# Moving some stationary operands by 128 bytes in SBUF, in a channel attention with a feed-forward layer

## The chip, the cores and the metric

The kernel runs on one core of a Trainium2 chip. The metric is the device time of one execution in microseconds (us). Before the change three runs gave 2107.0 us as their median, from 2104.4 to 2107.66.

## The reference

Two layers follow one another. The first is a channel attention: q, k and v are 4 batches of 6080 tokens by 256 channels. The second is a feed-forward layer with the square of a ReLU, of 256 channels and 2048 hidden ones, over all 24320 tokens.

```python
qn = q / (np.linalg.norm(q, axis=1, keepdims=True) + 1e-06)
kn = k / (np.linalg.norm(k, axis=1, keepdims=True) + 1e-06)
s = kn.transpose(0, 2, 1) @ qn / tau          # 256 x 256 per batch
a = np.exp(s - s.max(-1, keepdims=True))
a /= a.sum(-1, keepdims=True) + 1e-09
x = v @ a
h = np.maximum(x @ w_in, 0.0)
out = h * h @ w_out
```

The weights w_in and w_out come as 64-bit floating-point numbers, the rest as 32-bit ones.

## The kernel before

**Arithmetic.** Large products are made with the type fp32r, and each 32-bit operand is split into a high part and a low part; a product is three matmuls: high by high, high by low, low by high. Names ending in _hi and _lo are such parts. Since v @ a @ w_in is v @ (a @ w_in), each batch first makes its own W = a @ w_in, and the tokens then go through W, ReLU, square and w_out. The channels lie on the partitions, the tokens along the columns, so in the main loop weights are the stationary operand and tokens the moving one.

**Tiling.** A batch is 12 blocks of tokens: ten of 512 and two of 480. From the third block of the first batch on, both big products go by a scheme of two by two blocks with fewer products (like Strassen's), so that one matmul has half a block as columns: 256, or 240 in the last two blocks of a batch. The forms of W that it needs (with sums and differences of blocks) are kept in DRAM and loaded per group as the tiles wf. For w_out the plain blocks are read from wo_hi and wo_lo, and the sums from wS_hi, wS_lo (even pairs), wS_odd_hi, wS_odd_lo (odd pairs) and some blocks of wo that are overwritten. v is loaded as seven blocks in one tile (`load_v_blocks`, line 821): the places T1, B11, T3, B21, B22, T2, T4 are numbers 0 to 6 (line 986). In a tile of 240 columns they are 960 bytes apart, in one of 256 columns 1024.

**Order.** The loop over groups (four groups to a block of tokens, 512 hidden channels each) calls `period` (line 1331), which goes through the list PERIOD (line 1278): products with wf into the accumulators ps_b, ps_h and ps_c (`product`, line 991, six matmuls on one block of v), and between them the products with w_out of the two groups before into ps_o: `window_S` (line 1063) and `window_A` (line 1058). Every engine runs its instructions in the order of the program. ScalarE evicts, squares and makes high parts; VectorE adds, subtracts and makes low parts; both work beside TensorE. Beside the main loop, at places that `side` names, the attention of the next batch runs: its Gram matrix k-transposed by q (`Gram.products`, line 467; q and k split by `rounded_qk`, line 144, 12 matmuls to a chunk), its softmax (line 649) and its W, a product in which the exponentials eT are the stationary operand (line 751).

**Places in SBUF.** Pools are laid out one behind the other: smalls, const (with wo_hi, wo_lo), wpool (wf), wsums, pool. Within a pool each tag has its room, in the order in which the tags are first asked for. From wo_hi to the end of wsums all rooms are multiples of 1024 bytes per partition, and each begins at 192 modulo 256: wo, wf, wS (8192 bytes each part), wi_hi and wi_lo (4096 each, later the room of wS_odd), eT (2048 each). The first room of pool is that of the parts of q and k (`parts_room`, line 129), two halves of 4096 bytes with a gap between: `rounded_qk` puts k's parts into the first half, and q's parts HALF + GAP words behind them. With a gap of 64 bytes (line 127) the second half and all that follows in pool begin at 0 modulo 256: x, the loads of q and k, acc and dec (which later also hold w_in for the product with eT), A_hi and A_lo, v and its parts, s1 and s2 parts. So in the main loop the stationary operand begins at 192 and the moving one at 0 modulo 256, except that the blocks of 240 columns begin where multiples of 960 bytes fall. wsums holds these tags in this order: wS_hi, wS_lo, wi_hi, wi_lo, eT_hi, eT_lo.

Of the kernel before, what the change touches and what calls it, by code (L numbers as in the profile page):

```python
# [10 lines left out]
F32 = mybir.dt.float32  # L11
# [21 lines left out]
def kernel(  # L33
# [26 lines left out]
    P = 128  # L60
# [40 lines left out]
    wsums = ctx.enter_context(tc.tile_pool(name="wsums", bufs=1))  # L101
# [22 lines left out]
    rinv_room = const.tile([P, NC], F32, name="rinv_room")  # L124

    HALF = NC * GRP
    GAP = 16

    def parts_room(name, dt):

        return pool.tile([P, 2 * HALF + GAP], dt, tag="qk_parts", name=name, bufs=1)

    scalar.activation(parts_room("first", F32)[:, 0:1], exp_bias, AF.Square)
    wo_hi = const.tile([P, NF, C], F32R, name="wo_hi")
    wo_lo = const.tile([P, NF, C], F32R, name="wo_lo")
    late = {}

    def two_parts(name, dt, shape):

        room = parts_room(name, dt)  # L140
        halves = room[:, 0:HALF], room[:, HALF + GAP :]
        return [half.rearrange("p (a b) -> p a b", a=shape[1]) if len(shape) > 2 else half for half in halves]

    def rounded_qk(name):
# [3 lines left out]
        for at in (0, J * C):  # L148
            of_k = room[:, at : at + J * C]
            both = bass.AP(of_k.tensor, of_k.offset, [of_k.ap[0], [HALF + GAP, 2], of_k.ap[1]])  # L150
            parts.append(both.rearrange("p a (j c) -> p a j c", j=J))
# [1435 lines left out]
```

## Time and profile before

| | before |
|---|---|
| median of 3 runs | 2107.0 us (2104.4 to 2107.66) |
| profiled execution: its own time | 2107.39 us |
| its span | 2105.6 us |
| TensorE matmul busy | 2100.4 us (100%), 17158 instructions |
| VectorE busy | 1905.2 us (90%) |
| ScalarE busy | 1879.6 us (89%) |
| GpSimd busy | 350.2 us (17%) |
| DMA, mean | 261 GB/s |

The span runs from the first to the last instruction of the profiled execution, 1.8 us less than the execution's own time. Busy time is the sum of an engine's instructions without overlaps. Matmuls are pipelined, and a row gives one about 0.28 us though the next starts well before that is over; so what counts is the distance from one matmul's start to the next one's, which the chain of waits and the timeline give. The profile shows no addresses; those above are worked out from the sizes of the tiles and the order in which they are asked for.

### The profile page before, as it was taken

Reading aid. Unit: us, or ns where it says so; the run is one execution under the profiler, and the core shown is the slowest. Engines: PE = TensorE matmul, PEld = TensorE weight load, DVE = VectorE, ACT = ScalarE, POOL = GpSimd, SP = SyncE. Lnnn points to the kernel's source line nnn. Section 1 sums busy time; section 2 is a strip of 40 time slices with the busy share of each in tenths; the row PEclk is TensorE's granted clock in tenths of the full one; section 3 lists DMA queues with packets and bytes.
Section 4 is the critical chain, followed back from the end, with each engine's and each line's share of the span. In section 5 each row is a group of like instructions: output and inputs, shape, how many; then the busy total and the mean of one; then the engine's idle time right before and its main releaser. Section 6 shows DMA issues by size and latency. Waiting matters only on the chain.

```text
span 2105.6 us, 43463 instructions
## 1 busy us (share of the span) xinstructions
PE 2100.4 (100%) x17158; PEld 2065.7 (98%) x17158; DVE 1905.2 (90%) x2195; ACT 1879.6 (89%) x2379; POOL 350.2 (17%) x430
## 2 busy tenths in 40 slices
PE   9999999999999999999999999999999999999999
PEld 8789999999999999999999999999999999999999
DVE  7898999989999999989998999998999888888887
ACT  5888999889999999889989999998988988988987
POOL 0000111111121111111122111211111121121112
PEclk9999999999999999999999999999999999999999
DMA  9777888789999888788999978878999787787775
GB/s 357 224 230 274 247 267 250 243 253 309 307 278 317 257 247 255 237 253 281 292 299 277 308 251 260 247 243 248 287 278 304 233 239 246 235 242 243 232 242 154
DMA packets 258012, 549.78 MB, mean 261 GB/s; under 512 B 26672, under 2 KB 113072, under 8 KB 257808
## 3 DMA queue, kind: packets, MB, share of 16 engines
q1 hardware_dynamic: 201456, 469.02, 65.0%
q0 software_dynamic: 56352, 77.98, 18.6%
q8 instruction: 135, 2.21, 0.4%
q14 instruction: 69, 0.57, 0.1%
HBM read 433.59 MB, written 58.72 MB: 234 GB/s over the span
## 4 chain that ended last, share of the span: by engine, by line
PE 99%; ACT 0%; DVE 0%; issue 0%; DVEq 0%; ACTq 0%
PE ps_o L29 45%; PE ps_c L29 18%; PE ps_h L29 14%; PE ps_b L29 12%; PE gram L29 7%; PE ps_w L29 2%; PE ps_end L29 0%; PE ps_first L29 0%; PE ps_n L29 0%; ACT x L29 0%; PE ps_t L29 0%; DVE x L29 0%; DVE w_lo L29 0%; ACT A_hi L29 0%; ACT ps_c L29 0%
## 5 line engine op out<-in xcount | busy, mean ns | idle before, releaser
L29 PE MATMUL ps_c<-v_hi,wf 128*128 128x256 f32 (+1 forms) x2208 | 477.1, 279 | 0.3 <-DVE x L29 0.2
L29 DVE TENSOR_TENSOR x<-x 128x1024 f32<-128x1024 f32 (+2 forms) x549 | 464.9, 847 | 11.1
L29 POOL DMA_DIRECT2D o<-o x225 | 232.6, 1188 | 1401.6 <-ACT o L29 903.4
L29 DVE TENSOR_TENSOR s_lo<-x,s_hi 128x1024 fp32r<-128x1024 f32 (+1 forms) x366 | 441.2, 1207 | 16.6 <-ACT s_hi L29 16.2
L29 ACT ACTIVATE x<-x 128x1536 f32<-128x1536 f32 (+4 forms) x384 | 405.2, 1055 | 42.5 <-DVE x L29 38.9
L29 ACT CAST s_hi<-x 128x1024 fp32r<-128x1024 f32 (+1 forms) x366 | 382.3, 1044 | 50.1 <-DVE x L29 49.1
L29 DVE TENSOR_TENSOR A_lo<-x,A_hi 128x1536 fp32r<-128x1536 f32 (+2 forms) x183 | 313.5, 1713 | 83.1 <-ACT A_hi L29 75.0
L29 PEld LDWEIGHTS ps_c<-v_hi,wf 128*128 128x128 f32 x2208 | 375.4, 188 | 1.1 <-DVE x L29 0.4
L29 PE MATMUL ps_b<-v_hi,wf 128*128 128x256 f32 (+1 forms) x1472 | 317.3, 278 | 0.0
L29 PE MATMUL ps_h<-v_hi,wf 128*128 128x256 f32 (+1 forms) x1472 | 317.3, 278 | 0.0
L29 PE MATMUL ps_c<-v_lo,wf 128*128 128x256 f32 (+1 forms) x1104 | 307.5, 279 | 0.0
L29 ACT CAST A_hi<-x 128x1536 fp32r<-128x1536 f32 (+2 forms) x183 | 264.1, 1443 | 0.0
L29 PEld LDWEIGHTS ps_h<-v_hi,wf 128*128 128x128 f32 x1472 | 250.4, 188 | 0.0
L29 PEld LDWEIGHTS ps_b<-v_hi,wf 128*128 128x128 f32 x1472 | 250.3, 188 | 0.1
L29 PEld LDWEIGHTS ps_c<-v_lo,wf 128*128 128x128 f32 x1104 | 207.5, 188 | 0.1
L29 PE MATMUL ps_h<-v_lo,wf 128*128 128x256 f32 (+1 forms) x736 | 204.9, 278 | 0.0
L29 PE MATMUL ps_b<-v_lo,wf 128*128 128x256 f32 (+1 forms) x736 | 204.8, 278 | 0.0
L29 PE MATMUL ps_o<-A_hi,wo_hi 128*128 128x256 f32 (+1 forms) x897 | 193.3, 279 | 0.0
L29 PE MATMUL ps_o<-A_lo,wo_hi 128*128 128x256 f32 (+1 forms) x897 | 193.0, 279 | 0.0
L29 PE MATMUL ps_o<-A_hi,wo_lo 128*128 128x256 f32 (+1 forms) x897 | 192.6, 279 | 0.0
L29 ACT COPY x<-ps_c 128x512 f32<-128x512 f32 (+1 forms) x184 | 107.2, 582 | 53.1 <-PE ps_c L29 42.7
L29 PE MATMUL ps_o<-s_hi,wS_hi 128*128 128x256 f32 (+1 forms) x549 | 153.0, 279 | 0.0
(172 smaller groups left out, 5197.6 us busy)
## 6 DMA issues: line engine op xcount, KB each, us to landing
wf<-wf_kept SPq DMA_DIRECT2D x368, 512.0 KB, 5.2
wf<-wf_kept SPq DMA_DIRECT2D x368, 384.0 KB, 4.8
o<-o POOLq DMA_DIRECT2D x114, 256.0 KB, 5.0
qk<-in_k SPq DMA_DIRECT2D x88, 256.0 KB, 5.3
qk<-in_q SPq DMA_DIRECT2D x88, 256.0 KB, 5.4
v<-in_vT SPq DMA_DIRECT2D x76, 256.0 KB, 4.8
out_T<-o POOLq DMA_DIRECT2D x152, 128.0 KB, 5.1
wf_kept<-wS SPq DMA_DIRECT2D x64, 256.0 KB, 6.5
```

What stands on the lines that cost most here:

```text
L29: return lambda *args, **kwargs: self.tc.keep_in_program_order(issue(*args, **kwargs))
```

## The change

An unused tile of 32 words (128 bytes) is the first to be asked for in the pool wsums, and the gap between the halves of the room for the parts of q and k is 48 words (192 bytes) instead of 16 (64 bytes). So the tiles of wsums and the first half of the room for the parts begin at 64 modulo 256; the second half of that room and all tiles behind it move by 256 bytes and begin where they began modulo 256.

```diff
     HALF = NC * GRP
-    GAP = 16
+    GAP = 48
 
     def parts_room(name, dt):
...
     wo_hi = const.tile([P, NF, C], F32R, name="wo_hi")
     wo_lo = const.tile([P, NF, C], F32R, name="wo_lo")
+    wsums.tile([P, 32], F32, name="between")
     late = {}
```

## Rows read from the trace of the kernel before

**Rows 1.** The page: busy us, share, instructions; granted clock by fortieths in tenths.
```profile
PE 2100.4 (100%) x17158; PEld 2065.7 (98%) x17158; DVE 1905.2 (90%) x2195; ACT 1879.6 (89%) x2379; POOL 350.2 (17%) x430
...
PEclk9999999999999999999999999999999999999999
```

**Rows 2.** The page: the chain that ended last, by engine.
```profile
PE 99%; ACT 0%; DVE 0%; issue 0%; DVEq 0%; ACTq 0%
```

**Rows 3.** Waits of TensorE: who for whom, us in total, times, longest.
```profile
PE ps_first L29 <- DVE single L29: 1.1, 1, 1.1
```

**Rows 4.** Pieces of the chain: start us, us, what, matmuls.
```profile
173.38 2.12 PE ps_o L29 x18
...
269.99 1.41 PE ps_o L29 x12
...
286.94 1.41 PE ps_o L29 x12
295.43 1.41 PE gram L29 x12
```

**Rows 5.** Timeline of TensorE, two stretches: start us, us, operation, product<-operands, shape, count.
```profile
418.24 0.28 PE L29 MATMUL ps_o<-A_hi,wS_hi 128*128 128x256 f32 x1
...
418.92 0.28 PE L29 MATMUL ps_o<-A_hi,wo_hi 128*128 128x256 f32 x1
...
428.28 0.28 PE L29 MATMUL ps_o<-A_hi,wS_hi 128*128 128x256 f32 x1
...
428.99 0.40 PE L29 MATMUL ps_o<-A_hi,wo_hi 128*128 128x256 f32 x2
```

**Rows 6.** Timeline, 240 columns: first rows of T2, B21, T3, B22, T4, B11, T1 and what follows.
```profile
569.70 0.28 PE L29 MATMUL ps_c<-v_hi,wf 128*128 128x240 f32 x1
...
570.37 0.28 PE L29 MATMUL ps_b<-v_hi,wf 128*128 128x240 f32 x1
...
571.05 0.39 PE L29 MATMUL ps_o<-s_hi,wo_hi 128*128 128x240 f32 x2
...
572.39 0.27 PE L29 MATMUL ps_c<-v_hi,wf 128*128 128x240 f32 x1
...
573.07 0.28 PE L29 MATMUL ps_h<-v_hi,wf 128*128 128x240 f32 x1
...
573.74 0.39 PE L29 MATMUL ps_o<-A_hi,wo_hi 128*128 128x240 f32 x2
...
574.42 0.27 PE L29 MATMUL ps_c<-v_hi,wf 128*128 128x240 f32 x1
...
575.10 0.27 PE L29 MATMUL ps_o<-A_hi,wS_hi 128*128 128x240 f32 x1
...
576.44 0.27 PE L29 MATMUL ps_b<-v_hi,wf 128*128 128x240 f32 x1
...
577.11 0.28 PE L29 MATMUL ps_h<-v_hi,wf 128*128 128x240 f32 x1
...
577.78 0.27 PE L29 MATMUL ps_o<-s_hi,wS_hi 128*128 128x240 f32 x1
```

**Rows 7.** Weight loads by group: operation, product<-operands, shape, count, busy us, mean ns, idle before.
```profile
L29 PEld LDWEIGHTS ps_o<-s_lo,wS_hi 128*128 128x128 f32 x549 | 103.2, 188 | 0.0
...
L29 PEld LDWEIGHTS gram<-qk_parts 128*128 128x128 f32 x792 | 98.1, 188 | 0.0
...
L29 PEld LDWEIGHTS ps_o<-s_hi,wS_odd_hi 128*128 128x128 f32 x354 | 66.6, 188 | 0.0
...
L29 PEld LDWEIGHTS ps_o<-A_lo,wS_hi 128*128 128x128 f32 x183 | 34.5, 188 | 0.0
...
L29 PEld LDWEIGHTS ps_w<-dec_w,eT_lo 128*128 128x128 f32 x48 | 9.0, 188 | 2.1
...
L29 PEld LDWEIGHTS ps_w<-wi_lo_w,eT_hi 128*128 128x128 f32 x16 | 2.9, 188 | 1.0 <-DVE wi_lo_w L29 0.4
```

**Rows 8.** Timeline, the first 256-column products after a stretch of 240 columns.
```profile
585.87 0.28 PE L29 MATMUL ps_b<-v_hi,wf 128*128 128x256 f32 x1
...
586.58 0.28 PE L29 MATMUL ps_h<-v_hi,wf 128*128 128x256 f32 x1
...
587.28 0.28 PE L29 MATMUL ps_o<-s_hi,wS_hi 128*128 128x240 f32 x1
```

## The prediction

> **What bounds the kernel now.** I read first the page's part on busy time and its chain of waits. TensorE is busy for 2100.4 of 2105.6 us, and the chain that ended last runs through it for 99% of the span [rows 1, 2]. The longest of the waits that the trace puts to TensorE lasts 1.1 us, at the start [rows 3]. The granted clock stands at 9 tenths or more in all forty slices, so it is the 2.4 GHz level throughout [rows 1]. So the time is the number of matmuls times the distance between the starts of two of them: 2100.4 us over 17158 is 122 ns, 512-column and two-pass matmuls included. VectorE and ScalarE are 90% and 89% busy and hardly ever last to release TensorE.
>
> The chain's pieces then give that distance where only 256-column matmuls run: 2.12 us for 18 and 1.41 us for 12, both 117.6 ns [rows 4]. 256 columns at 2.4 GHz are 106.7 ns, so some 11 ns per matmul are something else, and nothing in the trace is waiting. The timeline shows what kind of thing it is. The same six matmuls (the second step of windows A: wS and wo in turn) take 0.71 us from 428.28 to 428.99, which is 118.3 ns each, and 0.68 us from 418.24 to 418.92, which is 113.3 ns each [rows 5]. The instructions, shapes and addresses are the same ones, and the clock is the same. So the stream of weight loads and matmuls holds one of at least two paces, and which one is a matter of how the two streams stand to each other. The lower pace is rare: the pieces of the chain of 12 and 18 matmuls are at 117.6.
>
> **Does the place in SBUF matter to that?** No row of this kernel has a stationary operand at 64 modulo 256 with its moving operand at 0, which is what the change makes. The nearest rows are the blocks of 240 columns: seven blocks of v lie 960 bytes apart, so block number 0 and 4 begin at 0, 1 and 5 at 192, 2 and 6 at 128, 3 at 64 modulo 256, all against weights at 192. A product is six matmuls on one block, and its time is the distance from its first row to the next step's [rows 6]. T2 0.67 us, B21 0.68, T3 0.68, B22 0.67, T4 0.68, B11 0.67, T1 0.67. Written as the distance from the moving to the stationary address modulo 256: 0 (T2, B11) and 192 (B22, T1) take 0.67, 128 (B21) and 64 (T3, T4) take 0.68. That is 0.01 us in six matmuls, 1.7 ns each; two starts, each rounded to 0.01 us, leave it between about 0 and 3.3 ns. So the place does matter a little, and the distance that the change brings, 64 in place of 192, is on the dear side in these rows.
>
> Here a rule of the Trainium skill speaks for no effect at all. "SBUF — State Buffer", section "Who interferes with whom", gives TensorE two independent read ports, one for the moving operand and one for the weights, and says that it never waits on anyone; by it the sum of this change is nothing. The two paces of rows 5 and the products of rows 6 do not fit that rule; it stays below as a rival's companion.
>
> **The change part by part.** (1) The tile "between" is never written or read, so it issues no instruction. It moves all that follows in its pool by 128 bytes: wS and wS_odd, the exponentials eT, and the wi tiles of the first batch, from 192 to 64. (2) The gap of 48 words instead of 16 makes the room for the parts of q and k 128 bytes longer. With the 128 in front that is 256, so all behind it keeps its place modulo 256, and so does the room's second half, from which q is read as the moving operand (0 before and after). The first half, the stationary k, goes to 64. No instruction, wait, DMA or order of a queue changes; what is moved past what stays as it is.
>
> TensorE's instructions that read the moved tiles as weights are, by the weight loads' counts [rows 7]: with wS three terms of 549 (sums) and three of 183 (windows A), with wS_odd three of 354, the Gram products of the later batches 792, and with eT three of 48 and three of 16. That is 1647 + 549 + 1062 + 792 + 192 = 4242, or 25% of all. The other 75% keep both addresses. So each nanosecond per affected matmul is 4.2 us, and that is just 0.2% of 2107.
>
> The price of one is unknown in the trace of before. Bounded below: all of them go at the lower pace, 113.3 instead of 117.7, which is -4.4 x 4242 = -18.7 us. Bounded above: the upper end of the product rows, +3.3 x 4242 = +14.0 us. By the rows' middle, 1.7 ns, it would be +7.2 us. I take +0.5 ns, +2.1 us, because a stream of 256 columns does not take over the differences of the 240-column one: right after the 240-column stretch, whose matmuls began at all four residues, the first two 256-column products take 0.71 and 0.70 us, 118.3 and 116.7, on average 117.5, the usual pace at once [rows 8]. The stream finds this pace from wherever it starts, and runs of at most 12 matmuls at the new place are followed by weights at 192 again.
>
> What else reads the moved tiles costs nothing: ScalarE writes the high parts and VectorE the low ones, both off the chain [rows 2], and TensorE's longest wait of 1.1 us is ahead of all of them [rows 3]; the cover is the lead by which these engines are early. Should each of them become longer, nothing in the chain moves until one is late at a matmul. The DMAs that save the first half of the parts start from another residue; the chain of waits holds none of them, so they cost nothing as long as no weights come late.
>
> The sum: 2107.39 us of the profiled execution (span 2105.6 and 1.8 around it) + 2.1 = 2109.5; the profiled execution lies 0.4 above the median 2107.0 of the runs, so against these it is 2109.1, and I say 2109.
>
> **The rivals.** (a) The new place is the better one: the affected matmuls go at 113.3. Rows 5 show that 256 columns can go at it with the same operands; against it, the stream left it and hardly ever found it. 2107.0 - 18.7 = 2088. If it also pulls the weights at 192 behind each run to the lower pace, it could be at most 4.4 ns on all 17158, 75 us: 2032. (b) Slower, by one mechanism: at distance 64 the reads of weights and of the moving operand meet more often, in every run of wS, wS_odd, eT and k, at the price of rows 6, 1.7 to 3.3 ns each: 2114 to 2121. It decides from 1.0 ns on, where 4242 of them make 4.2 us. For it are the three 0.68s; against it is that the 256-column stream goes back to one pace [rows 8]. (c) The address has no effect on TensorE at all: 2107.0, within the forecast's own case. It is what the page cited above would have. Against it speaks that B21, T3 and T4 are apart from the other four. (d) The change doesn't do what it says: an unused tile might get no room of its own. Then wS stays at 192 and all behind the parts lies at 128, so v and the squares are at distance 64 from all weights: 1.7 ns x 17158, 29 us, 2136.
>
> **How the numbers follow.** About 0.2%, 4.2 us, is what a measurement of this kernel can tell from no change. The forecast with (c), between -1.0 and +1.0 ns per affected matmul: 0.36. Case (a) for the affected alone 0.24, spread to others 0.06; together faster 0.30. Case (b) 0.31, (d) 0.03; together slower 0.34. The range goes from (a)'s 2088 to (b)'s upper end, 2122, and leaves out the spread of (a), (d) and a little beyond both ends, under 2 in 10. Cases of both signs hold most of the chance: the forecast's own range is 2103 to 2111.
>
> **What would show it.** In the changed profile, the second step of windows A (wS and wo in turn) and the 12-matmul runs of wS with wS_odd: 0.71 us per six is no change, 0.68 is (a), 0.72 and more is (b). The 12-matmul pieces of the Gram products in the chain: 1.41 us or not. The products with wf should stay at 0.70 to 0.71 per six; if they move, weights that keep their place have been pulled along. TensorE's count of 17158 and its waits should stay. The prediction is wrong if the affected matmuls move by over 1.0 ns, or the others by over 0.3.

## The result, and the profile after

The change made the kernel faster: 2070.51 us as the median of four runs (2070.11 to 2071.63) against 2107.19 us (2104.4 to 2107.66), a ratio of 0.9829 with a 95% interval of 0.9812 to 0.9846. The prediction was 2109 us, from 2088 to 2122; the result lies below that range. The profiled execution took 2070.66 us, with a span of 2068.8 us: 36.8 us less than before.

The page of the changed kernel first: busy us, share and instructions, the granted clock by fortieths, and the chain that ended last, by engine.

```profile
PE 2062.1 (100%) x17158; PEld 2021.1 (98%) x17158; DVE 1895.3 (92%) x2195; ACT 1870.7 (90%) x2379; POOL 350.5 (17%) x430
...
PEclk9999999999999999999999999999999999999999
...
PE 90%; DVE 5%; ACT 3%; issue 1%; DMA 0%; DVEq 0%; ACTq 0%; SPq 0%
```

The counts and the clock level are those of before [rows 1]; 17158 matmuls take 38 us less. And TensorE is no longer alone on the chain: 90% instead of 99% [rows 2], with VectorE and ScalarE behind it. So there are two things to find: a faster stream, and new waits.

The stream in two long stretches. Columns: stretch, its length, and for each engine the busy us and the instructions in it; then clock, DMA share and GB/s. First the kernel before, then the changed one.

```profile
600.00:1000.00 400.00, 400.00 (x3374) 398.91 (x3374) 371.00 (x411) 369.76 (x463) 71.49 (x87) 1.00 0.85 261
1800.00:2060.00 260.00, 260.00 (x2224) 260.00 (x2224) 227.22 (x243) 230.67 (x293) 49.12 (x60) 1.00 0.80 241
```

```profile
600.00:1000.00 400.00, 399.82 (x3472) 397.58 (x3471) 379.51 (x426) 376.98 (x474) 75.28 (x91) 1.00 0.89 269
1800.00:2060.00 260.00, 259.81 (x2263) 258.41 (x2262) 227.24 (x246) 231.36 (x297) 51.88 (x63) 1.00 0.77 231
```

At the same granted clock TensorE starts 98 more matmuls in the first of these stretches (3472 against 3374). The chain shows their pace, in pieces that answer to rows 4:

```profile
207.85 2.04 PE ps_o L29 x18
...
211.25 2.04 PE ps_o L29 x18
```

2.04 us over 18 is 113.3 ns, where 18 of rows 4 took 2.12, 117.8 ns each. The timeline shows that both paces are still there (start, us, operation, product<-operands, shape, count):

```profile
413.58 0.28 PE L29 MATMUL ps_o<-A_hi,wS_hi 128*128 128x256 f32 x1
...
414.26 0.39 PE L29 MATMUL ps_o<-A_hi,wo_hi 128*128 128x256 f32 x2
...
420.38 0.28 PE L29 MATMUL ps_c<-v_hi,wf 128*128 128x256 f32 x1
...
421.06 0.28 PE L29 MATMUL ps_h<-v_hi,wf 128*128 128x256 f32 x1
...
423.60 0.28 PE L29 MATMUL ps_o<-A_hi,wS_hi 128*128 128x256 f32 x1
...
424.31 0.40 PE L29 MATMUL ps_o<-A_hi,wo_hi 128*128 128x256 f32 x2
...
426.42 0.28 PE L29 MATMUL ps_o<-s_hi,wS_hi 128*128 128x256 f32 x1
...
427.13 0.28 PE L29 MATMUL ps_o<-s_hi,wS_hi 128*128 128x256 f32 x1
...
427.81 0.28 PE L29 MATMUL ps_c<-v_hi,wf 128*128 128x256 f32 x1
...
428.49 0.28 PE L29 MATMUL ps_b<-v_hi,wf 128*128 128x256 f32 x1
```

The second step of windows A takes 0.68 us for six at 413.58 and 0.71 at 423.60 as the two of before did [rows 5]. A product with wf, whose places did not change, takes 0.68 us at 420.38. At 421.75 four matmuls of another shape (ps_t) come between, and the stream is at 0.71 per six until 427.13; in the window in which wS_odd follows wS it falls back to 0.68, and the products with wf behind it stay there.

Over the whole trace, the distances were counted from the start of each 256-column matmul to the start of the next matmul (up to 115 ns low pace, 115 to 125 usual pace, above that a long distance). The 240 matmuls of the first batch's Gram matrix, whose operands are not split and which stand some 246 ns apart, are left out:

| | low pace | usual pace | long distances |
|---|---|---|---|
| before | 137 | 13421, mean 117.78 ns | 26, 5.7 us in all |
| after | 11090, mean 113.32 ns | 2372, mean 118.08 ns | 122, 27.6 us in all |

The matmuls that read moved tiles went from 117.76 to 114.00 ns on average without the long distances; 3487 of them have 256 columns, so that is 13.1 us. The 9972 that read wo and wf went from 117.73 to 114.25 ns: 34.8 us. The 96 more long distances give back 27.6 - 5.7 - 96 x 0.1178 = 10.6 us. The sum is 13.1 + 34.8 - 10.6 = 37.3 us, against the 36.8 us seen; 240-column matmuls hardly moved (112.20 and 112.28 ns).

What makes the long distances is seen in the chain after, for instance here (start us, us, what):

```profile
222.57 1.38 ACT A_hi L29
223.95 0.49 ACT x L29
224.44 0.04 issue
224.48 0.98 PE ps_c L29 x6
...
283.32 1.87 DVE x L29 x3
```

ScalarE and VectorE have their old instructions, but TensorE now uses up their results sooner; the product ps_c at 224.48 takes 0.98 us instead of 0.68. The view of waits puts only 2.5 us to TensorE in the changed kernel, so that the long distances are waits rests on this chain and on the run lighter below.

### The profile page after: what moved, and what is told of

The parts are those of the page before. It is cut to its first block, busy times and chain, and to the rows that moved or that the text cites. A ratio compares the mean times of both kernels' runs of the same rounds, so it can differ in the third digit from the quotient of the medians.

```text
span 2068.8 us, 43463 instructions
## 1 busy us (share of the span) xinstructions
PE 2062.1 (100%) x17158; PEld 2021.1 (98%) x17158; DVE 1895.3 (92%) x2195; ACT 1870.7 (90%) x2379; POOL 350.5 (17%) x430
## 4 chain that ended last, share of the span: by engine, by line
PE 90%; DVE 5%; ACT 3%; issue 1%; DMA 0%; DVEq 0%; ACTq 0%; SPq 0%
PE ps_o L29 40%; PE ps_c L29 17%; PE ps_h L29 13%; PE ps_b L29 11%; PE gram L29 6%; PE ps_w L29 2%; DVE x L29 2%; ACT x L29 1%; DVE A_lo L29 1%; DVE s_lo L29 1%; ACT A_hi L29 0%; DMA acc_w<-wi_kept 0%; ACT s_hi L29 0%; DVE v_lo L29 0%; DVE qk_parts L29 0%
## 5 line engine op out<-in xcount | busy, mean ns | idle before, releaser
L29 PE MATMUL ps_b<-v_hi,wf 128*128 128x256 f32 (+1 forms) x1472 | 311.3, 276 | 0.0
L29 PE MATMUL ps_h<-v_hi,wf 128*128 128x256 f32 (+1 forms) x1472 | 311.0, 276 | 0.0
L29 PE MATMUL ps_o<-s_lo,wS_hi 128*128 128x256 f32 (+1 forms) x549 | 151.9, 277 | 0.2 <-DVE s_lo L29 0.2
L29 PE MATMUL ps_o<-s_hi,wS_lo 128*128 128x256 f32 (+1 forms) x549 | 151.9, 277 | 0.0
```

The lines of the kernel that those rows point to most:

```text
L29: return lambda *args, **kwargs: self.tc.keep_in_program_order(issue(*args, **kwargs))
```

## The experiments

The first four runs were to tell apart whether the place 64 itself brings the low pace and pulls other weights along, or whether each matmul gains for itself, by the share that moved. From them came the theory of the cycle, which the later ones test: the stream can go at either pace, and a change of the weights' place throws it out of the usual one into the low one, in which it stays until something disturbs it.

"Place" is always the first byte modulo 256; moving operands are at 0 where nothing else is said. The kernel before, timed beside these runs, had medians from 2105.76 to 2107.33 us, and each ratio is to the one beside it. All edits but the last two kinds only add unused tiles or change the gap, so they issue no instruction.

| kernel | wo, wf | wS, wS_odd, eT | k | us | ratio, 95% | low pace | long |
|---|---|---|---|---|---|---|---|
| all_64 | 64 | 64 | 64 | 2082.22 | 0.988, 0.9841 to 0.9919 | 6338 | 57 |
| sums_128 | 192 | 128 | 128 | 2109.3 | 1.0017, 1.0006 to 1.0028 | 845 | 24 |
| only_k | 192 | 192 | 64 | 2085.11 | 0.9894, 0.9865 to 0.9922 | 6100 | 51 |
| only_eT | 192 | eT alone 64 | 192 | 2107.29 | 1.0009, 0.9998 to 1.002 | 104 | 26 |
| only_sums | 192 | 64 | 192 | 2071.12 | 0.9836, 0.9807 to 0.9864 | 10856 | 118 |
| swapped | 64 | 192 | 192 | 2069.8 | 0.9829, 0.9801 to 0.9858 | 12525 | 142 |
| shift_128, moving 128 | 64 | 192 | 192 | 2070.26 | 0.9831, 0.9803 to 0.986 | 11032 | 122 |
| more_changes | wo_hi 192; wo_lo, wf 64 | 192 | 192 | 2066.96 | 0.9816, 0.9787 to 0.9844 | 12490 | 148 |
| moving_128 | 192 | 192 | 192 | 2104.32 | 0.9989, 0.9978 to 0.9999 | 919 | 28 |
| sums_0 | 192 | 0 | 0 | 2083.94 | 0.9897, 0.9868 to 0.9926 | 7600 | 46 |
| all_128 | 128 | 128 | 128 | 2121.65 | 1.0076, 1.0047 to 1.0106 | 2573 | 21 |

**Is 64 simply the better place?** all_64 moves every weight to 64, where the change moves a quarter.

```diff
-    GAP = 16
+    GAP = 48
...
+    const.tile([P, 32], F32, name="ahead")
     wo_hi = const.tile([P, NF, C], F32R, name="wo_hi")
```

> Every stationary operand (wo, wf, wS, eT, the parts of k) begins at 64 modulo 256, the moving ones at 0 as before. Theory P (pull): at distance 64 the stream of matmuls settles at the lower pace of 113.3 ns by itself, at 192 it holds whichever of the two it has; then all 256-column stretches are at 113.3 here too and the time is 2060 to 2072 us. Theory M (mixture): it is the alternation of two places of the weights that breaks the pace of 117.7; with one place for all the pace is 117.7 again and the time is 2104 to 2110 us.

Measured 2082.22 us, so neither expectation held: one place for all weights brings 57% of the change's low pace (6338 of 11090) and some 24 of its 37 us. The low pace comes in long runs: of the matmuls number 4400 to 8050 in the order of the program, 3317 of the 3544 with 256 columns are at it, and 171 of 3210 from number 13200 to 16410, in the last batch. At 64 both paces stand for long. With one exception, wherever there are at least six matmuls at the one pace and then six at the other, a wait or matmuls of another shape lie between; the switches go both ways.

**Does a second place 64 bytes away do the same?** sums_128 moves the same tiles to 128 instead of 64: `GAP = 32`, and the tile `between` of 48 words (192 bytes).

> As the changed kernel, but wS, wS_odd, eT, wi of the first batch and the parts of k begin at 128 modulo 256 instead of 64; wo and wf stay at 192, moving operands at 0. Theory M: any second place breaks the pace of 117.7, so 2065 to 2080 us. Theory P makes no gain certain: it is a property of distance 64; if 128 has no pull, 2100 to 2115 us.

Measured 2109.3 us, 3.4 us above before: the distances scatter from 112 to 124 ns, and 845 matmuls are at the low pace, 8% of the change's.

**Which of the moved tiles?** only_k moves the parts of k alone, only_eT the exponentials alone, only_sums all of the pool wsums but not k.

```diff
# only_k
-    GAP = 16
+    GAP = 48
...
+    pool.tile([P, 32], F32, name="behind", bufs=1)
     scalar.activation(parts_room("first", F32)[:, 0:1], exp_bias, AF.Square)
# only_eT
+    pool.tile([P, 32], F32, name="behind", bufs=1)
...
+        if b == 0:
+            wsums.tile([P, 32], F32, name="between")
         eT_hi, eT_lo = (wsums.tile([P, NC, C], F32R, tag=f"eT_{i}", name=f"eT_{i}{b}", bufs=1) for i in ("hi", "lo"))
# only_sums
+    pool.tile([P, 32], F32, name="behind", bufs=1)
...
+    wsums.tile([P, 32], F32, name="between")
```

> Only the parts of k (792 Gram matmuls, 12 in a row) begin at 64 modulo 256; wS, wS_odd and eT stay at 192. Theory P: each run of 12 puts the stream to 113.3 and the matmuls after it, all at 192, keep it until TensorE next waits; so the stretches with Gram products gain nearly as in the changed kernel, the last batch (no Gram products) does not: 2078 to 2090 us. Theory S (share): only the moved matmuls themselves are faster, 792 of 4242 of the gain of 36.7 us, that is 7 us: 2098 to 2102 us.

> Only the exponentials eT (192 matmuls of 512 columns, in runs of 6 and 12) begin at 64 modulo 256. Theory P: if a few matmuls at 64 are enough and the pace is then kept, each product of W pulls the following stretch to 113.3; TensorE in the kernel before ran long stretches without a wait, the last batch (3200 matmuls behind the last eT) among them, so 2075 to 2100 us. Theory S: 192 matmuls, at most 2 us: 2105 to 2108 us.

> Only the tiles of wsums (wS, wS_odd, the exponentials, w_in's first tiles) go to 64 modulo 256; the parts of k stay at 192. Theory of the cycle (a change of the stationary place by 128 bytes throws the stream of 256-column matmuls from the 117.8 ns pace into the 113.3 ns pace, in which it then stays): windows with wS alternate with wo and wf in the whole main loop, so nearly the same as with the change: 2068 to 2082 us, over 9000 matmuls at 113.3. Theory that the parts of k do it (they alone gave 22 us): the rest of the change has the other part only, 2085 to 2100 us and no 113.3 in the last batch, where there is no Gram product left.

only_k came out as theory P had it, only_sums as the theory of the cycle, only_eT as theory S. only_k is the plainest of all. It moves 792 matmuls and takes 20.8 us off, 26 ns for each, where the two paces are 4.5 ns apart: most of it must be other matmuls. The chain (start us, us, product, matmuls), in the second batch and in the last one, which has no Gram products:

```profile
902.50 0.68 PE ps_c L29 x6
903.18 0.68 PE ps_h L29 x6
...
1851.98 0.71 PE ps_c L29 x6
1852.69 0.71 PE ps_h L29 x6
```

Both are products with wf at 192 and v at 0. At 902.50 they are at 113.3 ns, at 1851.98 at 118, and no matmul from number 13200 on is at the low pace. After the 512-column products of the first batch, the stream goes from the usual to the low pace, for at least eight matmuls, at 13 places. Nine of them lie at or in a run of k's parts, with no wait or other shape between; the other four lie right behind a wait or behind matmuls of another shape, with all weights at 192. So the moved weights start the low pace, and others keep it, but a disturbance can start it too. only_eT started hardly any (104 at the low pace, as few as before): its matmuls have 512 columns, and behind matmuls of another shape the stream is at either pace. The changed kernel's chain, and then only_k's:

```profile
909.05 0.68 PE ps_h L29 x6
909.73 1.39 PE ps_w L29 x6
911.12 0.71 PE ps_o L29 x6
```

```profile
913.18 0.71 PE ps_h L29 x6
913.89 1.39 PE ps_w L29 x6
915.27 0.68 PE ps_o L29 x6
```

The exponentials' product ps_w stands between six at 113.3 ns and six at 118 in the one, and the other way round in the other, where it reads weights at 192 as its neighbours do. So what starts the low pace in the main loop are wS and wS_odd: only_sums gives the whole effect, in the last batch as well, and k adds nothing to it that can be measured. The theory by which k carried the gain fell here.

**The place, or the change of it?** swapped gives wo and wf the new place and leaves the sums. shift_128 moves everything in the changed kernel by 128 bytes. more_changes makes the places change within every window and product.

```diff
# swapped: GAP stays 16
+    const.tile([P, 32], F32, name="ahead")
     wo_hi = const.tile([P, NF, C], F32R, name="wo_hi")
     wo_lo = const.tile([P, NF, C], F32R, name="wo_lo")
+    wsums.tile([P, 32], F32, name="between")
# shift_128: the same two, and
-    GAP = 16
+    GAP = 48
# more_changes: as swapped, but
     wo_hi = const.tile([P, NF, C], F32R, name="wo_hi")
+    const.tile([P, 32], F32, name="ahead")
     wo_lo = const.tile([P, NF, C], F32R, name="wo_lo")
```

> The places change roles: wo and wf begin at 64, wS, wS_odd, the exponentials and the parts of k at 192 modulo 256, all moving operands stay at 0. Theory of the cycle: only the difference of 128 bytes between weights that follow one another counts, 2065 to 2082 us, over 9000 matmuls at 113.3. Theory that 64 is the better place for the sums, and worth something to those alone: the sums are back where they were, 2100 to 2110 us; if each weight at 64 were better for itself, the 75% that moved would bring three times as much as the change, under 2040 us.

> Everything of the changed kernel from wo_hi on is moved by 128 bytes: wo and wf at 64, wS, wS_odd, the exponentials and the parts of k at 192, and the moving operands at 128 modulo 256. The differences are those of the change, every place by itself is another. If only differences count: 2068 to 2074 us and about 11000 matmuls at 113.3. If places count by themselves: off by more than 8 us from the change's 2070.5, in either direction.

> wo_hi stays at 192, wo_lo goes to 64, wf goes to 64; wS, wS_odd, the exponentials and the parts of k stay at 192: the place of the weights changes within every window and product, more often than with the change. Theory of the cycle: the stream comes back into the 113.3 ns pace sooner after each wait, so not slower than the change, 2055 to 2073 us, and over 11000 matmuls at 113.3. Rival, that the number of changes has nothing to do with it and each change costs something: 2075 to 2107 us.

All three came out as the theory of the cycle had it, and outside the ranges of the others: with wS, wS_odd and k where they were before, the gain is the same (swapped), and so it is with every place another by 128 bytes (shift_128). In all three the weights still come from 192 and 64. The last batch of more_changes, beside the two rows of this stretch above:

```profile
1800.00:2060.00 260.00, 259.77 (x2263) 257.82 (x2262) 227.29 (x251) 227.78 (x292) 51.82 (x63) 1.00 0.76 228
```

It is as far as the changed kernel there, though more of its matmuls are at the low pace: what is gained in pace beyond that is lost in waits.

**Is it the distance between moving and stationary operand?** moving_128 leaves all weights at 192 and puts the parts of S1 and S2 to 128, so the distance changes by 128 bytes from window to window without a change of the weights' place.

```diff
+        if not G:
+            pool.tile([P, 32], F32, name="ahead", bufs=1)
         hi, _ = G[b, n, r] = [
```

> The kernel before, all weights at 192, but the parts of S1 and S2 (moving operands of the windows with the sums) begin at 128 modulo 256 instead of 0; A and v stay at 0. If what counts is the distance between the moving and the stationary operand, and that it changes by 128 bytes between successive runs: the same kind of gain, 2065 to 2085 us. If what counts is that the weights come from two places: nothing, 2104 to 2109 us.

Measured 2104.32 us: 3 us of 37, and 919 matmuls at the low pace. In the last batch the chain keeps the usual one:

```profile
1848.83 1.41 PE ps_o L29 x12
```

But 762 of the 919 read the parts of S1 and S2. Behind products ps_w, for instance, a window of A (first row, moving operand at 0) and one of S (second row, at 128):

```profile
462.75 1.41 PE ps_o L29 x12
...
465.57 1.37 PE ps_o L29 x12
```

Of 304 windows of S, 55 have most of their matmuls at the low pace (2 of 304 before), 51 of them from 446 to 518, from 934 to 1036 and from 1451 to 1553 us. 47 of the 55 go to it right behind six matmuls at the usual pace, with every weight at 192, and the products behind them, with v at 0, go back. So a change of the moving operand's place can start the low pace too, but hardly outside these three stretches, and it does not last. For most of the 37 us the weights have to come from different places.

**Which differences do?** sums_0 is 64 bytes apart as sums_128 was, the other way (`GAP = 0`, the tile `between` of 16 words). all_128 is a third place for all weights (`GAP = 32`, the tile `ahead` of 48 words).

> The tiles of wsums and the parts of k begin at 0, wo and wf at 192, the moving operands at 0 modulo 256: the weights come from two places 64 bytes apart, as in sums_128, but the other way. If 128 bytes between the places are needed: 2100 to 2110 us, fewer than 1500 matmuls at 113.3. If any change of place does it and sums_128 failed for another reason: 2065 to 2085 us.

> All weights begin at 128 modulo 256, the moving operands at 0. If the lower pace needs weights from two places: 2095 to 2110 us, with the low pace in a minority of the matmuls, and none in the last batch for long. If a place by itself can be good (all at 64 gave half of the gain): 2065 to 2085 us.

sums_0 took 2083.94 us, within the range of "any change of place". The timeline of TensorE in the last batch:

```profile
1852.59 0.28 PE L29 MATMUL ps_o<-s_hi,wS_hi 128*128 128x256 f32 x1
...
1853.31 0.28 PE L29 MATMUL ps_c<-v_hi,wf 128*128 128x256 f32 x1
...
1853.99 0.28 PE L29 MATMUL ps_h<-v_hi,wf 128*128 128x256 f32 x1
```

The six with wS and wS_odd, weights and moving operand both at 0, take 0.72 us, 120 ns each; the six with wf behind them 0.68, 113.3 ns. So the products in which the low pace is left cost more here, but weights that go from 0 to 192 bring it back, and about four in five of the matmuls with wf are at it: 128 bytes are not needed, and that part of the theory fell. all_128 was slower than before by 15.9 us, which neither side had. Its pieces of the chain:

```profile
1845.37 1.43 PE ps_o L29 x12
...
1852.49 1.43 PE ps_o L29 x12
```

1.43 us over 12 is 119 ns. With the moving operand at 0 a weight at 128 is dear; of the 2573 that the table counts as low pace, 2527 stand 115 ns apart, not 113. sums_128 has the same dear matmuls, 118.6 to 119.1 ns on average where one at 128 follows another, but its products with wf at 192 stay at 117.8: why going from 128 to 192 does not bring the low pace, as going from 0 to 192 does, no run shows.

**What takes part of the gain back?** lighter leaves out the last of VectorE's three sums of each group. add_first lets VectorE add ps_c, which frees it for TensorE, ahead of the double sum. Both start from the changed kernel.

```diff
# lighter, in last_sum
-        vector.tensor_sub(x[:, :, a3, :], x[:, :, a3, :], x[:, :, a2, :])
+        return
# add_first, in PERIOD
-        (1, two_sums),
         (2, lambda k: copy_output(k, 1)),
         (None, "sq"),
         (0, second_H),
         (0, add_C),
+        (1, two_sums),
```

> The changed kernel with VectorE's last of three sums of each group left out (183 instructions, so the result lacks that sum); every matmul, address and ScalarE instruction stays. If the gain given back (some 11 us) is TensorE's wait for VectorE and ScalarE, which the lower pace makes late: fewer than 60 distances over 125 ns in place of 122, and 2060 to 2066 us. If TensorE makes those long distances by itself: 2069 to 2072 us.

> The changed kernel, but VectorE adds ps_c into x ahead of the double sum instead of behind it, so TensorE's next product into ps_c is released earlier. If that sum is what makes TensorE wait there: the long distances ahead of that product go (26 in the last batch and 14 before it), 2064 to 2070 us. If VectorE then idles until ps_c is complete (0.8 us in each of 183 groups, against some 170 us of room) and is late elsewhere: 2072 to 2100 us.

lighter took 2063.71 us, ratio 0.9796 (0.9778 to 0.9814), within its range: taking work from VectorE gives back 8.7 us against the change timed beside it (2072.41), or 6.8 against the first 2070.51, though TensorE's own work is the same. Its chain:

```profile
PE 99%; DVE 0%; ACT 0%; issue 0%; DVEq 0%; ACTq 0%
```

83 long distances are left, not the fewer than 60 that were expected: up to the last batch 30 instead of 69, in the last batch 53 as in the changed kernel. There they come at the start of the fourth product into ps_c, which waits for this in the changed kernel (VectorE, then TensorE):

```profile
1850.16 1.23 DVE L29 TENSOR_TENSOR x<-x 128x1024 f32<-128x1024 f32 x1
1851.30 0.68 DVE L29 CUSTOM_DVE_ANT_0 x<-x,ps_c 128x512 f32<-128x512 f32 x1
```

```profile
1851.77 0.39 PE L29 MATMUL ps_o<-A_lo,wo_hi 128*128 128x256 f32 x2
1852.04 0.39 PE L29 MATMUL ps_c<-v_hi,wf 128*128 128x256 f32 x1
```

The addition that reads ps_c ends at 1851.98, the product starts at 1852.04; the double sum ahead of it is work that lighter does not touch. add_first was meant to take that away, and took 2158.95 us, ratio 1.0253 (1.0224 to 1.0283), far beyond the 2072 to 2100 of its worse case. VectorE's additions from ps_c, with the idle time ahead of them (us, and whom it waited for), in the changed kernel and in add_first:

```profile
L29 DVE CUSTOM_DVE_ANT_0 x<-x,ps_c 128x512 f32<-128x512 f32 x152 | 103.5, 681 | 9.6 <-PE ps_c L29 6.5 <-ACT x L29 2.7 <-ACT qk L29 0.3
```

```profile
L29 DVE CUSTOM_DVE_ANT_0 x<-x,ps_c 128x512 f32<-128x512 f32 x152 | 104.4, 687 | 68.7 <-PE ps_c L29 54.1 <-ACT v_hi L29 4.1 <-ACT o L29 3.7
```

The double sum had been standing in time in which VectorE would wait for ps_c anyway. Moved behind, it leaves 59 us of idle time in these 152 places (and 21 us in the 32 of 240 columns), and VectorE, 92% busy in the changed kernel, does not make it up: VectorE and ScalarE hold 28% of add_first's chain instead of 8%.

**The version with more changes, timed beside the change.** Both ran on one chip in turn, four and five times.

> The kernel with wo_lo and wf at 64 and all else at 192, once more, in more rounds beside the changed kernel. Theory of the cycle: 2066 to 2068 us, 3 to 5 us below the changed kernel; if the look before was luck, the two agree within 2 us.

> The change as it is, in the same rounds, as the measure for the kernel with more changes of place: 2070 to 2072 us.

2067.3 us (2066.55 to 2068.54), ratio 0.9814 (0.98 to 0.9827), against 2072.41 us (2070.39 to 2074.18), ratio 0.9837 (0.9824 to 0.985), for the change. No run of the one reaches the other. So changing the place within each window beats the change by some 5 us; the change itself lay 0.4 us above its expected 2070 to 2072.

## Why the prediction was wrong

- **The bound was right, and the two paces too.** TensorE's stream set the time, and the pace of 256-column matmuls was the whole matter [rows 1, 2, 4, 5]. (2.12 us over 18 is 117.8 ns and 1.41 over 12 is 117.5; the 117.6 given for both lies between, and the trace's mean is 117.8. That the pace is a matter of how two streams stand to each other was argued there, and no run shows it.)
- **The step that failed** is the price of the moved matmuls: "+0.5 ns", because "the stream finds this pace from wherever it starts" [rows 8]. Measured: -3.8 ns for each of the 3487 with 256 columns, which is -13.1 us instead of +2.1. Rows 8 show products with wf alone, one place for all six weights, and such a stream does keep the usual pace. They say nothing on a stream whose weights change place. And "from wherever it starts" went against the stretch of rows 5 itself: there, with all weights at 192, 75 matmuls from 417.68 to 426.3 us keep the low pace. After the change the stretch of rows 8 behaves the same (two products from 580.28 to 581.70, 0.71 us each), and still the rest of the kernel got faster:

```profile
580.28 0.28 PE L29 MATMUL ps_b<-v_hi,wf 128*128 128x256 f32 x1
...
580.99 0.28 PE L29 MATMUL ps_h<-v_hi,wf 128*128 128x256 f32 x1
...
581.70 0.27 PE L29 MATMUL ps_o<-s_hi,wS_hi 128*128 128x240 f32 x1
```

- **A second step failed, and it weighs more:** the other 75%, which "keep both addresses", were put at nothing. They moved by -3.5 ns, -34.8 us, nearly three quarters of the gain in pace. That was rival (a) in its spread form, at a chance of 0.06 and 2032 us; the mechanism came, at half of its price, because 2494 of 13584 256-column matmuls stay at the usual pace or wait, wider ones and those of 240 columns have no part in it, and 10.6 us went to the new waits. The prediction gave (a) 0.30 in all; its bound of -18.7 us for the affected alone was sound (-13.1).
- **Rival (b)**, a dearer place, is wrong for 64 and right for others: all weights at 128 cost 15.9 us. The products of rows 6 gave the sign for a 240-column stream and did not carry over to 256 columns at 64.
- **Rival (c)**, no effect of addresses, falls. It was the companion of the Trainium skill's "SBUF — State Buffer", section "Who interferes with whom", by which the two read ports of TensorE are independent; the measured 113.3, 117.8 and 119 to 120 ns, with the same instructions at other addresses, disagree with what was drawn from it there. Whether the ports themselves are independent, no run shows.
- **Rival (d)** falls: runs that differ by unused tiles and gaps alone took from 2067 to 2122 us, so unused tiles do move the others.
- **"TensorE's count and its waits should stay"**: the count did, the waits did not: the lead of VectorE and ScalarE was enough at 117.8 ns and is used up at 113.3.

What the runs show of the mechanism: one place for all weights (192, 64) lets both paces stand, and with 192 the stream is nearly always at the usual one. A change of the weights' place between 192 and 64, or from 0 to 192, brings it to 113.3 ns, and it stays there over weights that keep their place. In the changed kernel a wait or a matmul of another shape ends it, and the next changes bring it back. Elsewhere such a disturbance also starts it (only_k, all_64), so it rather leaves the stream at either pace. In the changed kernel the stream goes 50 times from at least six matmuls at the usual pace straight to six at the low one, and at all 50 the weights' place changes within three matmuls, as it does at 46% of all its matmuls; the kernel before has no such start. Why a change of the weights' place does this for good, when one of the moving operand's did it for one window at a time and only in some stretches, and why the weights at 64 find the low pace so much oftener than those at 192, stays open: the traces show starts, not what happens within a matmul. Pairs of places other than 192 with 64, 128 or 0 were not run.

## What to carry to other kernels

Where the chain is a stream of equal matmuls, compare the same group of instructions at two times: if it has two paces without any wait, the stream has a state, and the price of an edit is not its own instructions times a difference, but the state it leaves to all that follows. Try weights in two places, with the change inside each run, before giving up nanoseconds per matmul as fixed, and try more than one pair: 192 with 64 gained 37 us here, 192 with 128 lost 3. And a faster bound uses up the cover of the next engines: count their room at the new pace, not at the old one.

## What the runs showed of the hardware

- 256-column matmuls of this type, at the 2.4 GHz level throughout, run at 113.3 or 117.8 ns with the same instructions and addresses, and at 119 to 120 where the weights begin at 128 or 0 with the moving operand at 0. By the Trainium skill's "TensorE: Matmul & The Clock Gate", section "Wait — 56ns, not 53.3ns?", columns over 2.4 GHz and about 2.5 ns would be an estimated 109.2 ns; no stretch here comes down to that.
- 792 matmuls with weights in another place took 20.8 us off a kernel of 17158 (only_k).
- Weights all at 192, moving operands at 0 and 128 in turn: in 55 of 304 windows at 128 the stream went to the low pace, and back at the next product at 0 (moving_128).
- A VectorE instruction of 1.2 us that stood ahead of one that waits for TensorE used time that VectorE would have waited; moving it behind cost 88 us against the change (add_first).
